# First values loaded in eight pieces by head to 64 partitions each, with the first loads' order and VectorE's first steps rearranged

## The chip, the cores and the metric

The kernel runs on one core of a Trainium2 chip. The metric is the device time of one execution in microseconds. Before the change it is 104.87 us, the median of three runs (104.6 to 105.11).

## The reference

A sketched polynomial attention, and behind it a two-layer block. All inputs and the output are float32.

```python
# q, k, v: (batch 4, heads 4, seq 1088, head_dim 32); S1, S2: (8, 32)
def phi(x):
    a = np.einsum('rd,bhsd->bhsr', S1, x)
    b = np.einsum('rd,bhsd->bhsr', S2, x)
    return np.einsum('bhsi,bhsj->bhsij', a, b).reshape(*x.shape[:-1], 64)
q_p, k_p = phi(q), phi(k)
kv = np.einsum('bhsf,bhsd->bhfd', k_p, v)
z = np.sum(k_p, axis=2)
x = einsum('bhsf,bhfd->bhsd', q_p, kv) / (einsum('bhsf,bhf->bhs', q_p, z)[..., None] + 1e-06)
# x as (4352 tokens, 128 = heads * head_dim); w_in: (128, 2048), w_out: (2048, 128)
h = x @ w_in
out = (h - np.tanh(h)) @ w_out
```

## The kernel before, in words

The four batches are worked through one after the other. A sequence of 1088 positions is cut into 34 blocks of 32, position `j * 34 + c` being row j of block c; a key or query tile holds (head, j) on 128 partitions and (block, dimension) along them. For each batch the kernel loads the keys (`kraw`), turns them in 32x32 blocks on VectorE (`kT`, two halves, L514), multiplies them on TensorE by the sketch (`kp`, L525) and turns the result (`kab`, L531). The products of the two sketches are `wk` (L545, in pieces on VectorE and GpSimd). TensorE sums `wk` times the values `vx` over the sequence (`sum`, L581); the result is spread by ScalarE (`kvz`, L591), turned by TensorE (`turn`, L601) and stored as the weights `ndw` (L608). The queries (`qraw`) are turned (`qT`, L620), projected (`qp`; L643 for the first 12 blocks, L660 for the others), normalized (`qab`, `au`, `dn`, `rd`, `an`), multiplied out (`qm`, L684), turned (`qt`, L691) and multiplied by `ndw` (`num`, L706). That gives `xT`, the input of the second part (L729).

The second part takes groups of 8 to 16 blocks: products with 16 slices of `w_in` (`h`, L778), tanh of the negative on ScalarE (`t`, L781), and the sum with 16 slices of `w_out` (`o`, L829). The linear share of the output comes from the product of the two weight matrices (`wp`, `whi`, `wlo`, L747 to L752, L821).

The order of the work is written out by hand: `ORDERS` lists the steps of each engine's program, `SESSIONS` the turns of the PSUM banks. `GATES` holds added dependences: `a<b` lets step a start after step b. Steps on SyncE are loads and stores in the order in which its queue issues them; ScalarE issues a few loads as well (`VENG` and `KENG` name which). In TensorE's list `~52`, `*4`, `^1` and the like stand for matmuls of constants, whose results nobody reads.

The tile `vx` has (block group ct, j) on its 128 partitions and, for each head, up to 9 blocks of 32 dimensions along them. The groups have 9, 9, 8 and 8 blocks (`KS`). Before the change `load_v` fills 32 partitions for all four heads with one load, `v0.0` to `v0.3` for the first batch. `sum0.0` (block places 0 to 3) and `sum0.4` (places 4 to 8) wait for all pieces of the first values. The load `wo0` of half of `w_out` is gated on `sum0.4`.

Of the kernel before, what the change touches and what calls it, by code (L numbers as in the profile page):

```python
# [14 lines left out]
NJB = DFF // 128  # L15
# [25 lines left out]
class Program:  # L41
# [241 lines left out]
k0.1 s1 act0 v0.2 v0.3 kap0 qab0 wq0u wic0 kvz0 ndw0 wic2 wic3 x0.0 t2 t3 t13 t11 t15 t14 t0 t1 t9 t5 t4 t12 t10 t8 t6
t7 x1.0 x1.2 t30 t22 t20 t18 t19 t32 t31 t47 t24 t16 t17 t42 t25 t23 t21 t29 t28 t27 t26 t39 t34 t38 t43 t46 t33 kvz1
t35 t40 t45 ndw1 t36 t44 t37 t41 t51 t49 t53 t48 t64 t50 t57 t52 t54 t59 t55 t65 t63 t58 t56 t60 t61 t62 t66 t67 t69
t68 kvz2 t72 t74 t70 ndw2 t78 t73 t71 t75 t76 t77 t84 t79 t87 t85 t80 t81 t109 t83 t90 t101 t88 t108 t82 t86 t93 t103
t89 t91 t105 t92 t94 t95 t96 kvz3 t111 t97 t98 ndw3 t110 t100 t99 t106 t104 t102 t112 t107 t116 t118 t114 t124 t122
t120 t128 t130 t126 t134 t132 t140 t138 t136 t146 t144 t142 t148 t150 t152 t154 t156 t158 out9.1 st9
# [13 lines left out]
s2 k0.0 q0.1 q0.0 q0.2 v0.1 v0.0 wi0 wi2 wi3 wi1 k1.0 wo0 wo1 wT q1.0 k2.0 v1.0 v1.1 v1.2 v1.3 st1.0.0 st1.0.3 q2.0
v2.2 v2.3 st0.0.2 st0.0.1 st0.0.3 st0.0.0 v2.0 st2.0.2 st2.0.3 v2.1 st1.0.1 v3.1 st2.0.0 st1.0.2 v3.3 st2.0.1 v3.0
k3.0 v3.2 st3.0.2 q3.0 st3.0.0 st3.0.1 st4.0.1 st3.0.3 st4.0.3 st5.2.2 st5.0.1 st5.2.3 st4.0.2 st5.2.0 st4.0.0 st5.0.0
st5.2.1 st6.0.1 st5.0.3 st6.0.3 st5.0.2 st7.0.2 st6.0.2 st7.4.2 st6.0.0 st7.4.1 st7.4.3 st7.0.0 st7.0.1 st7.4.0
st8.0.3 st8.0.0 st8.0.2 st7.0.3 st8.0.1
""",
}

# [10 lines left out]


GATES = """
id0<hm4.3 kTz0<hm4.3 kTz1<qT0.0 vz0<sel au1.0<bmask au1.1<bmask wqz<kp0 qTz0<hm4 qTz1<wq0 vz1<wq q0.0<hm2 v0.0<identb
v0.2<au1.1 v0.3<vz1 wi0<wkm wi1<qab0 wi2<wqz wi3<kTz1 q0.2<hm4 k1.0<qpu0 v1.0<o11 v1.1<h25 v1.2<t25 v1.3<o23
wo0<sum0.4 wo1<wic2 q1.0<t0 wic1<num0.0 woc0<kT1.0 wk0.29<wq0 qm0.2<dn0 wk1.12<o9 wk1.30<o13 k2.0<o9 v2.0<h64 v2.1<o35
v2.2<o4 v2.3<wk1.12 q2.0<qt2.2 au2<h23 an2<o22 qm2.2<t26 wk2.12<qab3 wk2.30<o33 k3.0<t66 v3.0<h49 v3.1<t50 v3.3<h60
q3.0<h30 wk3.12<o78 au4<o82 an4<t86 qm4.2<o86
"""


def bass_polysketch_attn__then__act_tanh_shrink_kernel(nc, q, k, v, S1, S2, moe_w_in, moe_w_out, out):
# [17 lines left out]
    def dve(n):  # L349
        return 45 + n / 0.96  # L350
# [70 lines left out]
    def constants():  # L421
        T = -9e5
        P.op("act0", "scalar", 1300, lambda e: e.copy(junk[:, :], nc.const_aps.tensor(1.0, [128, 1], BF16)), w=[("junk",)], prio=T)
        P.op("hm4", "vector", 70, lambda e: e.memset(hm4[:, :], 0.0), w=[("hm4",)], prio=T + 1)
        for h in range(H):
            P.op(f"hm4.{h}", "vector", 70, lambda e, h=h: e.memset(hm4[32 * h:32 * h + 32, h:h + 1], 1.0),
                 w=[("hm4",)], prio=T + 1)
        P.op("hm2", "vector", 80, lambda e: e.tensor_tensor(
            out=hm2[:, :], in0=hm4[:, 0:2], in1=hm4[:, 2:4], op=ALU.add), r=[("hm4",)], w=[("hm2",)], prio=T + 2)
# [15 lines left out]
        P.op("identb", "gpsimd", 250, lambda e: e.tensor_copy(identb[:, :], ident[:, :]), r=[("ident",)], w=[("identb",)], prio=T + 5)
# [23 lines left out]
    def load_v(b, eng, prio):  # L469
        i = b % 2  # L470
        src = v[b].rearrange("h (j c) d -> j h c d", j=32)
        for ct, (c0, n) in enumerate(KS):
            P.op(f"v{b}.{ct}", VENG.get((b, ct), eng), 0, lambda e, ct=ct, c0=c0, n=n: e.dma_start(
                out=vx[i][32 * ct:32 * ct + 32, :, 0:n, :].rearrange("j h t d -> j h (t d)"),
# [151 lines left out]
    def q_front(u, b, c0, nc_, early, bk):  # L626
# [4 lines left out]
        first = [c0 + sum(own[:ct]) for ct in range(4)]  # L631
        n = 4 * m
        cols = sorted({c for ct in range(4) for c in range(first[ct], min(first[ct] + m, 34))})
        need = [("qT", i, c) for c in cols] + ([("qTz", i)] if first[3] + m > 34 else [])
        if early:
            def project(x0, x1, base):
                def fn(e):
                    for t in range(m):
                        for c in range(2):
# [4 lines left out]
                    return ins  # L644
                return fn

            held = bank(f"qp{u}", bk)
            P.op(f"qp{u}", "tensor", pef(2 * m, 64, 64, 2), project(0, 16, 0), r=[("wq0",)] + need, w=held, ins=8 * m)
            pq = ps[:, bk, 0:16 * n].rearrange("p (n x) -> p n x", x=16)
            pu = ps[:, bk, 16 * n:24 * n].rearrange("p (n x) -> p n x", x=8)  # L650
            P.op(f"qab{u}", "scalar", act(16 * n), lambda e: e.copy(qab[ui][:, 0:n, 0:16], pq), r=held, w=[("qab", ui)])
            P.op(f"qpu{u}", "tensor", pef(2 * m, 64, 32, 2), project(16, 24, 16 * n), r=[("wq0u",)] + need, w=held, ins=8 * m)
        else:
            b0 = QBASE.get(u, 0)
            banks = range(b0, b0 + H)
# [1 line left out]
            def project(e):  # L657
# [100 lines left out]
    def layers(g, p0, nb, when):  # L758
# [2 lines left out]
        pace = PACE * n / 512  # L761
        slot = n_slot[0]
        n_slot[0] += NJB
        for jb in range(0, NJB, 2) if g in PAIRG else ():
            s = slot + jb
            b0, ts, at = (PBANKS if g not in ROWS else PBANKS[1:])[n_pair[0] % (len(PBANKS) - (g in ROWS))], s % TSLOTS, when + pace * jb
            n_pair[0] += 1
            for y in range(2):
# [3 lines left out]
            P.op(f"t{s}", "scalar", act(2 * n), lambda e, ts=ts, b0=b0: e.activation(  # L772
                out=tt[:, ts:ts + 2, 0:n], in_=ps[:, b0:b0 + 2, 0:n], func=AF.Tanh, scale=-1.0),
                r=bank(f"h{s}", b0, b0 + 1), w=[("t", ts), ("t", ts + 1)], prio=at)
        for jb in range(NJB) if g not in PAIRG else ():
            s = slot + jb
            bk, ts, at = 4 + s % NHB, s % TSLOTS, when + pace * jb
            P.op(f"h{s}", "tensor", pe(n), lambda e, jb=jb, bk=bk: e.matmul(  # L778
# [154 lines left out]
```

## Time and profile before

| what | value |
|---|---|
| median of the runs | 104.87 us (104.6 to 105.11) |
| the profiled execution: time, span from first to last instruction | 104.0 us, 102.2 us |
| TensorE matmul busy | 93.5 us (91%) |
| ScalarE busy | 79.6 us (78%) |
| VectorE busy | 54.8 us (54%) |
| GpSimd busy | 34.1 us (33%) |
| chain that ended last | TensorE 62%, GpSimd 11%, DMA 10%, VectorE 9% |
| DMA | 11.74 MB, mean 115 GB/s over the span |
| VectorE waiting for TensorE's sums of the second layer (L829) | 17.1 us |

A busy share is a mean over stages with different limits. The chain that ended last follows the work back from the last instruction to what released each step, and so tells which engine or load held the end in each stage. The page's row of DMA shares over 40 slices of the span shows the loads at nine tenths and more in the slices from 2.6 us on, at the start of the program, and far lower in the rest.

### The profile page before, as it was taken

To read this page: it belongs to the slowest core of one execution; us is meant where nothing else is said; L and a number is where in the kernel's file an instruction comes from. 1 tells how busy PE (TensorE), PEld (TensorE's weight loads), DVE (VectorE), ACT (ScalarE), POOL (GpSimd) and SP (SyncE) were. 2 spreads that over 40 slices of the span, in tenths; PEclk is the share of its full clock that TensorE was granted. 3 is DMA by queue.
4 is the path that set the end of the run, shared out by engine and by line. 5 is a ranking of instruction groups with operands and counts; after the bars stand their busy time and mean duration, and the time that the engine had idled before them with its cause. 6 is when DMAs were issued, how large, how long until landed. Compare 5 with 4: busy or idle time off the path is not lost.

```text
span 102.2 us, 3184 instructions
## 1 busy us (share of the span) xinstructions
PE 93.5 (91%) x1365; PEld 49.3 (48%) x1377; DVE 54.8 (54%) x95; ACT 79.6 (78%) x156; POOL 34.1 (33%) x41
## 2 busy tenths in 40 slices
PE   6978969999999989999999999999899999999950
PEld 6725642457444754433464344444443444456740
DVE  2589988885586765973086884830756020020210
ACT  2203579877998693999899779999776999999940
POOL 3138322834438950019980000569900000000000
PEclk9999999999999999999999999999999999999999
DMA  2999989954432139247579400130045003006242
GB/s 56 333 270 243 286 282 266 206 199 133 149 88 76 22 89 301 37 93 163 129 234 232 106 6 0 31 46 0 6 67 86 2 0 58 0 7 108 32 76 75
DMA packets 25949, 11.74 MB, mean 115 GB/s; under 512 B 19792, under 2 KB 24400, under 8 KB 25936
## 3 DMA queue, kind: packets, MB, share of 16 engines
q1 hardware_dynamic: 25320, 10.89, 44.0%
q10 hardware_dynamic: 616, 0.66, 2.3%
q8 instruction: 10, 0.16, 0.7%
q14 instruction: 3, 0.02, 0.1%
HBM read 8.79 MB, written 2.23 MB: 108 GB/s over the span
## 4 chain that ended last, share of the span: by engine, by line
PE 62%; POOL 11%; DMA 10%; DVE 9%; issue 3%; SPq 1%; POOLq 0%; DVEq 0%
PE ps L829 22%; PE ps L778 14%; PE ps L769 8%; POOL qp L684 8%; DMA w_out_f<-in_moe_w_out_dram 6%; PE ps L706 6%; DMA qraw<-in_q_dram 4%; PE ps L821 3%; DVE qpT L691 2%; PE ps L581 2%; PE ps L660 2%; PE ps L794 2%; DVE wk L545 2%; DVE qab L666 1%; DVE qT L620 1%
## 5 line engine op out<-in xcount | busy, mean ns | idle before, releaser
L781 ACT ACTIVATE tt<-ps 128x512 bf16<-128x512 f32 (+2 forms) x112 | 53.6, 549 | 7.8 <-PE ps L778 5.3
L829 PE MATMUL ps<-tt,w_out 128*128 128x512 bf16 (+3 forms) x141 | 39.7, 355 | 0.6 <-POOL w_out L738 0.3
L778 PE MATMUL ps<-xT,w_in 128*128 128x512 bf16 (+2 forms) x106 | 33.3, 353 | 1.7 <-ACT xT L729 0.6
L829 PEld LDWEIGHTS ps<-tt,w_out 128*128 128x128 bf16 x144 | 13.9, 99 | 12.2 <-ACT tt L781 0.8
L772 ACT ACTIVATE tt<-ps 128x1024 bf16<-128x1024 f32 (+2 forms) x24 | 18.6, 866 | 0.1
L778 PEld LDWEIGHTS ps<-xT,w_in 128*128 128x128 bf16 x112 | 10.2, 97 | 17.0 <-ACT tt L781 10.1
L684 POOL TENSOR_TENSOR qp<-an,qab 128x1152 f32<-128x1152 f32 (+2 forms) x8 | 15.4, 1926 | 1.9 <-DVE an L677 1.2
L691 DVE STREAM_TRANSPOSE qpT<-qp 128x1152 f32<-128x1152 f32 (+2 forms) x10 | 11.2, 1129 | 7.9 <-POOL qp L684 7.8
L834 DVE STREAM_TRANSPOSE osb<-ps 128x512 f32<-128x512 f32 (+3 forms) x9 | 5.8, 648 | 17.8 <-PE ps L829 17.1
L545 POOL TENSOR_TENSOR wk<-kab 128x384 f32<-128x384 f32 (+2 forms) x8 | 9.0, 1127 | 14.5 <-PE ps L829 14.0
L769 PE MATMUL ps<-xT,w_in 128*128 128x512 bf16 (+2 forms) x48 | 12.4, 335 | 0.0
L706 PE MATMUL ps<-qpT,ndw 32*32 32x288 f32 (+4 forms) x320 | 6.9, 352 | 0.4 <-DVE qpT L691 0.3
L729 DVE CAST xT<-ps 128x576 bf16<-128x576 f32 (+2 forms) x7 | 4.4, 682 | 4.7 <-PE ps L706 4.7
L769 PEld LDWEIGHTS ps<-xT,w_in 128*128 128x128 bf16 x48 | 4.4, 97 | 4.7 <-ACT tt L772 1.4
L671 POOL TENSOR_TENSOR au<-qab 128x288 f32<-128x288 f32 x3 | 2.4, 792 | 12.0 <-DVE qab L666 10.3
L514 DVE STREAM_TRANSPOSE kT<-kraw 128x512 f32<-128x512 f32 (+1 forms) x8 | 5.8, 720 | 0.8 <-DMA kraw<-in_k_dram 0.8
L620 DVE STREAM_TRANSPOSE qT<-qraw 128x1088 f32<-128x1088 f32 (+2 forms) x5 | 5.4, 1072 | 1.3 <-DMA qraw<-in_q_dram 1.3
L666 DVE STREAM_TRANSPOSE qab<-ps 128x1152 f32<-128x1152 f32 (+1 forms) x4 | 5.1, 1282 | 0.9 <-PE ps L660 0.7
L706 PEld LDWEIGHTS ps<-qpT,ndw 32*32 32x32 f32 x320 | 4.1, 103 | 2.9 <-DVE qpT L691 1.2
L581 PE MATMUL ps<-wk,vx 128*32 128x64 f32 x288 | 4.9, 220 | 0.5 <-DVE wk L545 0.5
L581 PEld LDWEIGHTS ps<-wk,vx 128*32 128x32 f32 x288 | 4.2, 110 | 1.4 <-issue 1.4
L416 PE MATMUL ps<-const-bfloat16-1.0 128*32 128x256 bf16 x77 | 3.9, 372 | 0.8 <-PEq L918 0.8
(82 smaller groups left out, 76.3 us busy)
## 6 DMA issues: line engine op xcount, KB each, us to landing
kraw<-in_k_dram SPq DMA_DIRECT2D x3, 544.0 KB, 4.1
qraw<-in_q_dram SPq DMA_DIRECT2D x3, 544.0 KB, 4.5
vx<-in_v_dram SPq DMA_DIRECT2D x8, 144.0 KB, 2.9
w_in_f<-in_moe_w_in_dram SPq DMA_DIRECT2D x4, 256.0 KB, 4.3
w_out_f<-in_moe_w_out_dram SPq DMA_DIRECT2D x2, 512.0 KB, 5.9
vx<-in_v_dram SPq DMA_DIRECT2D x6, 128.0 KB, 3.1
out_dram<-osb SPq DMA_DIRECT2D x12, 64.0 KB, 2.0
out_dram<-osb SPq DMA_DIRECT2D x12, 48.0 KB, 2.0
```

What stands on the lines that cost most here:

```text
L545: P.op(f"wk{b}.{n0}", eng, (dve if eng == "vector" else pool)(64 * n), lambda e, n0=n0, n1=n1, n=n, a_=a_: e.tensor_tensor(out=wk[0][:, n0 ...
L581: ins = e.matmul(ps[32 * h:32 * h + 32, SB, 0:64], vx[i][:, h, t, :], wk[0][:, 4 * t + h, :], start=(t == 0), stop=(t == 8), tile_position ...
L620: P.op(f"qT{b}.{lo}", "vector", dve(32 * (hi - lo)), lambda e: e.transpose(out=dst, in_=src), r=[("qraw", i, c) for c in range(lo, hi)], w ...
L666: P.op(f"qab{u}", "vector", dve(32 * n), lambda e: e.transpose(out=qab[ui][:, 0:n, :].rearrange("p (h t) x -> p h t x", h=H), in_=ps[:, b0 ...
L684: P.op(f"qm{u}.{h0}", eng, (pool if eng == "gpsimd" else dve)(64 * (n1 - n0)), lambda e, n0=n0, n1=n1, b_=b_: e.tensor_tensor(out=qp[ui][: ...
L691: P.op(f"qt{u}.{h0}", "vector", dve(64 * (n1 - n0)), lambda e, n0=n0, n1=n1: e.transpose(out=qpT[ui][:, n0:n1, :, :].rearrange("p n y j -> ...
L706: ins = e.matmul(ps[32 * h:32 * h + 32, ct, 0:32 * own[ct]], ndw[i][32 * ct:32 * ct + 32, y, 32 * h:32 * h + 32], qpT[ui][32 * ct:32 * ct ...
L769: P.op(f"h{s + y}", "tensor", pe(n), lambda e, jb=jb, b0=b0, y=y: e.matmul(ps[:, b0 + y, 0:n], w_in[:, 128 * (jb + y):128 * (jb + y) + 128 ...
L772: P.op(f"t{s}", "scalar", act(2 * n), lambda e, ts=ts, b0=b0: e.activation(out=tt[:, ts:ts + 2, 0:n], in_=ps[:, b0:b0 + 2, 0:n], func=AF.T ...
L778: P.op(f"h{s}", "tensor", pe(n), lambda e, jb=jb, bk=bk: e.matmul(ps[:, bk, 0:n], w_in[:, 128 * jb:128 * jb + 128], xT[:, t0:t0 + n], star ...
L781: P.op(f"t{s}", "scalar", act(n), lambda e, ts=ts, bk=bk: e.activation(out=tt[:, ts, 0:n], in_=ps[:, bk, 0:n], func=AF.Tanh, scale=-1.0), ...
L829: P.op(f"o{slot + jb}", "tensor", pe(n), lambda e, jb=jb, ts=ts: e.matmul(acc[:, 0:n], w_out[:, jb, :], tt[:, ts, 0:n], start=late and jb ...
```

## The change

The values of the first batch (`VHEADS`) are loaded in eight pieces, one for each head and each half of the partitions: 64 partitions of one head, two block groups of 32 partitions side by side. Four pieces go out on SyncE's queue and four on ScalarE's. The gates on these loads and on two of the query loads are removed (`q0.0<hm2`, `v0.0<identb`, `v0.2<au1.1`, `v0.3<vz1`, `q0.2<hm4`), as is the gate `kTz1<qT0.0` of a fill on GpSimd. The query pieces `q0.0` and `q0.1` are issued in the order of their blocks. VectorE turns both halves of the first keys and then copies the sketches (`wkm`, `wq`, `s2f`, `wq0`), turns the projected keys and then the queries. TensorE's two runs of constant matmuls at the start get three and four more. The zero fill behind `qT` is 64 columns wide instead of 32. The diff also holds further paths (`PAIR1`, `PSG`, `BU`, and a split turn of the queries) that no list or size of this kernel uses.

```diff
-VENG = {(0, 2): 'scalar', (0, 3): 'scalar'}
+VENG = {(0, 4): 'scalar', (0, 5): 'scalar', (0, 6): 'scalar', (0, 7): 'scalar'}
+VHEADS = (0,)
 ORDERS = {
     "tensor": """
-~52 sk ~25 kp0 *4 gram0 qp0 fold0 ...
+~55 sk ~29 kp0 *4 gram0 qp0 fold0 ...
     "scalar": """
-k0.1 s1 act0 v0.2 v0.3 kap0 qab0 ...
+k0.1 s1 act0 v0.4 v0.5 v0.6 v0.7 kap0 qab0 ...
     "vector": """
-hm4 hm4.0 hm4.1 hm4.2 hm4.3 hm2 sel bmask kT0.2 wkm wq kT0.0 s2f qT0.0 wq0 kab0 qT0.12 gm0 ...
+hm4 hm4.0 hm4.1 hm4.2 hm4.3 hm2 sel bmask kT0.2 kT0.0 wkm wq s2f wq0 kab0 qT0.0 qT0.12 gm0 ...
     "sync": """
-s2 k0.0 q0.1 q0.0 q0.2 v0.1 v0.0 wi0 wi2 wi3 wi1 k1.0 wo0 wo1 ...
+s2 k0.0 q0.0 q0.1 q0.2 v0.0 v0.1 v0.2 v0.3 wi0 wi2 wi3 wi1 k1.0 wo0 wo1 ...
 GATES = """
-id0<hm4.3 kTz0<hm4.3 kTz1<qT0.0 vz0<sel ... q0.0<hm2 v0.0<identb
-v0.2<au1.1 v0.3<vz1 wi0<wkm wi1<qab0 wi2<wqz wi3<kTz1 q0.2<hm4 k1.0<qpu0 ...
+id0<hm4.3 kTz0<hm4.3 vz0<sel ... wi0<wkm wi1<qab0 wi2<wqz
+wi3<kTz1 k1.0<qpu0 ...
 def load_v(b, eng, prio):
     i = b % 2
     src = v[b].rearrange("h (j c) d -> j h c d", j=32)
+    if b in VHEADS:
+        for x in range(2 * H):
+            h, (p0, c0, n) = x % H, ((0, 0, 9), (64, 18, 8))[x // H]
+            P.op(f"v{b}.{x}", VENG.get((b, x), eng), 0, lambda e, h=h, p0=p0, c0=c0, n=n: e.dma_start(
+                out=vx[i][p0:p0 + 64, h, 0:n, :].rearrange("p t d -> p (t d)"),
+                in_=v[b, h].rearrange("(j c) d -> j c d", j=32)[:, c0:c0 + 2 * n, :].rearrange("j (x t) d -> x j (t d)", x=2)),
+                w=[("vx", i)], sem=f"v{i}" + ("a" if (b, x) in VENG else ""), prio=prio, size=64 * 128 * n, also=True)
+        return
```

More of the change, by code (lines that the diff above doesn't have):

```diff
@@ L259 @@
 KENG = {(0, 1): 'scalar'}
-VENG = {(0, 2): 'scalar', (0, 3): 'scalar'}
+VENG = {(0, 4): 'scalar', (0, 5): 'scalar', (0, 6): 'scalar', (0, 7): 'scalar'}
 AENG = {2: 'gpsimd', 3: 'gpsimd', 4: 'gpsimd'}
+VHEADS = (0,)
+PAIR1 = ()
+PSG = ()
+BU = {}
 ORDERS = {
     "tensor": """
-~52 sk ~25 kp0 *4 gram0 qp0 fold0 *1 ^1 qpu0 sum0.0 sum0.4 *2 turn0 ^1 qp1 num0.0 num0.1 !1 h2 h3 h13 h11 h15 h1 h14
+~55 sk ~29 kp0 *4 gram0 qp0 fold0 *1 ^1 qpu0 sum0.0 sum0.4 *2 turn0 ^1 qp1 num0.0 num0.1 !1 h2 h3 h13 h11 h15 h1 h14
 h0 kp1 h9 h5 o0 h4 o1 o2 h12 gram1 o3 h10 h8 fold1 o4 o5 h6 h7 num1.0 num1.1 o6 o7 o8 o9 o10 h30 o11 h20 o12 o13 h22
@@ L282 @@
     "scalar": """
[L283 to L288, printed above, removed]
+k0.1 s1 act0 v0.4 v0.5 v0.6 v0.7 kap0 qab0 wq0u wic0 kvz0 ndw0 wic2 wic3 x0.0 t2 t3 t13 t11 t15 t14 t0 t1 t9 t5 t4 t12
+t10 t8 t6 t7 x1.0 x1.2 t30 t22 t20 t18 t19 t32 t31 t47 t24 t16 t17 t42 t25 t23 t21 t29 t28 t27 t26 t39 t34 t38 t43 t46
+t33 kvz1 t35 t40 t45 ndw1 t36 t44 t37 t41 t51 t49 t53 t48 t64 t50 t57 t52 t54 t59 t55 t65 t63 t58 t56 t60 t61 t62 t66
+t67 t69 t68 kvz2 t72 t74 t70 ndw2 t78 t73 t71 t75 t76 t77 t84 t79 t87 t85 t80 t81 t109 t83 t90 t101 t88 t108 t82 t86
+t93 t103 t89 t91 t105 t92 t94 t95 t96 kvz3 t111 t97 t98 ndw3 t110 t100 t99 t106 t104 t102 t112 t107 t116 t118 t114
+t124 t122 t120 t128 t130 t126 t134 t132 t140 t138 t136 t146 t144 t142 t148 t150 t152 t154 t156 t158 out9.1 st9
 """,
     "vector": """
-hm4 hm4.0 hm4.1 hm4.2 hm4.3 hm2 sel bmask kT0.2 wkm wq kT0.0 s2f qT0.0 wq0 kab0 qT0.12 gm0 wk0.8 wk0.0 wk0.16 au0 dn0
+hm4 hm4.0 hm4.1 hm4.2 hm4.3 hm2 sel bmask kT0.2 kT0.0 wkm wq s2f wq0 kab0 qT0.0 qT0.12 gm0 wk0.8 wk0.0 wk0.16 au0 dn0
 rd0 an0 qm0.0 wqu0 qt0.0 qt0.2 qab1 au1 dn1 rd1 kT1.0 an1 kT1.2 qm1.0 kab1 qt1.0 gm1 qt1.2 wqu1 wk1.24 wk1.0 qT1.0 whi
@@ L301 @@
     "sync": """
[L302 to L306, printed above, removed]
+s2 k0.0 q0.0 q0.1 q0.2 v0.0 v0.1 v0.2 v0.3 wi0 wi2 wi3 wi1 k1.0 wo0 wo1 wT q1.0 k2.0 v1.0 v1.1 v1.2 v1.3 st1.0.0
+st1.0.3 q2.0 v2.2 v2.3 st0.0.2 st0.0.1 st0.0.3 st0.0.0 v2.0 st2.0.2 st2.0.3 v2.1 st1.0.1 v3.1 st2.0.0 st1.0.2 v3.3
+st2.0.1 v3.0 k3.0 v3.2 st3.0.2 q3.0 st3.0.0 st3.0.1 st4.0.1 st3.0.3 st4.0.3 st5.2.2 st5.0.1 st5.2.3 st4.0.2 st5.2.0
+st4.0.0 st5.0.0 st5.2.1 st6.0.1 st5.0.3 st6.0.3 st5.0.2 st7.0.2 st6.0.2 st7.4.2 st6.0.0 st7.4.1 st7.4.3 st7.0.0
+st7.0.1 st7.4.0 st8.0.3 st8.0.0 st8.0.2 st7.0.3 st8.0.1
 """,
@@ L322 @@
 GATES = """
[L323 to L327, printed above, removed]
+id0<hm4.3 kTz0<hm4.3 vz0<sel au1.0<bmask au1.1<bmask wqz<kp0 qTz0<hm4 qTz1<wq0 vz1<wq wi0<wkm wi1<qab0 wi2<wqz
+wi3<kTz1 k1.0<qpu0 v1.0<o11 v1.1<h25 v1.2<t25 v1.3<o23 wo0<sum0.4 wo1<wic2 q1.0<t0 wic1<num0.0 woc0<kT1.0 wk0.29<wq0
+qm0.2<dn0 wk1.12<o9 wk1.30<o13 k2.0<o9 v2.0<h64 v2.1<o35 v2.2<o4 v2.3<wk1.12 q2.0<qt2.2 au2<h23 an2<o22 qm2.2<t26
+wk2.12<qab3 wk2.30<o33 k3.0<t66 v3.0<h49 v3.1<t50 v3.3<h60 q3.0<h30 wk3.12<o78 au4<o82 an4<t86 qm4.2<o86
 """
@@ L372, in bass_polysketch_attn__then__act_tanh_shrink_kernel @@
     kT = [sb(f"kT{i}", [128, 9, 4, 32]) for i in range(2)]
-    qT = [sb(f"qT{i}", [128, 35 * 32]) for i in range(2)]
+    qT = [sb(f"qT{i}", [128, 36 * 32]) for i in range(2)]
     vx = [sb(f"vx{i}", [128, H, 9, D]) for i in range(2)]
@@ L447, in constants @@
         for i in range(2):
-            P.op(f"qTz{i}", "gpsimd", 170, lambda e, i=i: e.memset(qT[i][:, 34 * 32:35 * 32], 0.0), w=[("qTz", i)], prio=T + 7)
+            P.op(f"qTz{i}", "gpsimd", 170, lambda e, i=i: e.memset(qT[i][:, 34 * 32:36 * 32], 0.0), w=[("qTz", i)], prio=T + 7)
         P.op("vz1", "gpsimd", 250, lambda e: e.memset(vx[1][64:128, :, 8, :], 0.0), w=[("vz", 1)], prio=T + 8)
@@ L615, in q_turned @@
         i = b % 2
+        if early and (hi - lo) % 4 == 2:
+            m = (hi - lo + 2) // 4
+            to = qT[i][:, 32 * lo:32 * (lo + 4 * m)].rearrange("p (t c j) -> p c t j", c=4, j=32)
+            for c, at, n in ((0, lo, m), (2, lo + 2 * m, m - 1)):
+                P.op(f"qT{b}.{at}", "vector", dve(64 * n), lambda e, c=c, at=at, n=n: e.transpose(
+                    out=to[:, c:c + 2, 0:n, :], in_=qraw[i][:, 32 * at:32 * (at + 2 * n)].rearrange("p (c t j) -> p c t j", c=2, j=32)),
+                    r=[("qraw", i, x) for x in range(at, at + 2 * n)], w=[("qT", i, x) for x in range(at, at + 2 * n)])
+            return
         dst, src = qT[i][:, 32 * lo:32 * hi], qraw[i][:, 32 * lo:32 * hi]
@@ L633, in q_front, with project @@
         cols = sorted({c for ct in range(4) for c in range(first[ct], min(first[ct] + m, 34))})
-        need = [("qT", i, c) for c in cols] + ([("qTz", i)] if first[3] + m > 34 else [])
+        need = [("qT", i, c) for c in cols] + ([("qTz", i)] if first[3] + m > 34 or (early and nc_ % 4) else [])
         if early:
-            def project(x0, x1, base):
+            def project(x0, x1, base, bk):
                 def fn(e):
@@ L645, in project @@
                 return fn
-            held = bank(f"qp{u}", bk)
-            P.op(f"qp{u}", "tensor", pef(2 * m, 64, 64, 2), project(0, 16, 0), r=[("wq0",)] + need, w=held, ins=8 * m)
+            held, hu, bu = bank(f"qp{u}", bk), bank(f"qp{u}", bk), bk
+            ub = 16 * n
+            if u in BU:
+                bu, ub = BU[u], 0
+                hu = bank(f"qp{u}", bu)
+            P.op(f"qp{u}", "tensor", pef(2 * m, 64, 64, 2), project(0, 16, 0, bk), r=[("wq0",)] + need, w=held, ins=8 * m)
             pq = ps[:, bk, 0:16 * n].rearrange("p (n x) -> p n x", x=16)
-            pu = ps[:, bk, 16 * n:24 * n].rearrange("p (n x) -> p n x", x=8)
+            pu = ps[:, bu, ub:ub + 8 * n].rearrange("p (n x) -> p n x", x=8)
             P.op(f"qab{u}", "scalar", act(16 * n), lambda e: e.copy(qab[ui][:, 0:n, 0:16], pq), r=held, w=[("qab", ui)])
-            P.op(f"qpu{u}", "tensor", pef(2 * m, 64, 32, 2), project(16, 24, 16 * n), r=[("wq0u",)] + need, w=held, ins=8 * m)
+            P.op(f"qpu{u}", "tensor", pef(2 * m, 64, 32, 2), project(16, 24, ub, bu), r=[("wq0u",)] + need, w=hu, ins=8 * m)
         else:
@@ L668, in q_front @@
                 in_=ps[:, b0:b0 + H, 0:32 * m].rearrange("p h (t j) -> p h t j", j=32)), r=bank(f"qp{u}", *banks), w=[("qab", ui)])
-            pq, pu, held = qab[ui][:, 0:n, :], qab[ui][:, 0:n, 16:24], []
+            pq, pu, held, hu = qab[ui][:, 0:n, :], qab[ui][:, 0:n, 16:24], [], []
         src = held + [("qab", ui)]
         P.op(f"au{u}", AENG.get(u, "vector"), (dve if u not in AENG else pool)(8 * n) + 30, lambda e: e.tensor_tensor(
-            out=au[ui][:, 0:n, 0:8], in0=qab[ui][:, 0:n, 0:8], in1=pu, op=ALU.mult), r=src, w=[("au", ui)], lock=not early)
+            out=au[ui][:, 0:n, 0:8], in0=qab[ui][:, 0:n, 0:8], in1=pu, op=ALU.mult), r=hu + src, w=[("au", ui)], lock=not early)
         P.op(f"dn{u}", "vector", dve(9 * n) + 30, lambda e: e.tensor_reduce(
@@ L763, in layers @@
         n_slot[0] += NJB
+        for jb, m in ((0, 2), (2, 1), (3, 2), (5, 1), (6, 2), (8, 1), (9, 2), (11, 1), (12, 2), (14, 1), (15, 1)) if g in PSG else ():
+            s = slot + jb
+            bk, ts, at = 4 if m == 2 or jb == 15 else 6, s % TSLOTS, when + pace * jb
+            for y in range(m):
+                P.op(f"h{s + y}", "tensor", pe(n), lambda e, jb=jb, bk=bk, y=y: e.matmul(
+                    ps[:, bk + y, 0:n], w_in[:, 128 * (jb + y):128 * (jb + y) + 128], xT[:, t0:t0 + n], start=True, stop=True),
+                    r=[("w_in", (jb + y) // 4)] + xs, w=bank(f"h{s}", bk + y), prio=at - 1000, ins=4)
+            P.op(f"t{s}", "scalar", act(m * n), lambda e, ts=ts, bk=bk, m=m: e.activation(
+                out=tt[:, ts:ts + m, 0:n], in_=ps[:, bk:bk + m, 0:n], func=AF.Tanh, scale=-1.0),
+                r=bank(f"h{s}", *range(bk, bk + m)), w=[("t", ts + y) for y in range(m)], prio=at)
+        for jb in range(0, NJB, 2) if g in PAIR1 else ():
+            s = slot + jb
+            bk, ts, at = 4 + (s // 2) % NHB, s % TSLOTS, when + pace * jb
+            for y in range(2):
+                P.op(f"h{s + y}", "tensor", pe(n), lambda e, jb=jb, bk=bk, y=y: e.matmul(
+                    ps[:, bk, n * y:n * y + n], w_in[:, 128 * (jb + y):128 * (jb + y) + 128], xT[:, t0:t0 + n], start=True, stop=True),
+                    r=[("w_in", jb // 4)] + xs, w=bank(f"h{s}", bk), prio=at - 1000, ins=4, also=y == 1)
+            P.op(f"t{s}", "scalar", act(2 * n), lambda e, ts=ts, bk=bk: e.activation(
+                out=tt[:, ts:ts + 2, 0:n], in_=ps[:, bk, 0:2 * n].rearrange("p (y n) -> p y n", y=2), func=AF.Tanh, scale=-1.0),
+                r=bank(f"h{s}", bk), w=[("t", ts), ("t", ts + 1)], prio=at)
         for jb in range(0, NJB, 2) if g in PAIRG else ():
@@ L774, in layers @@
                 r=bank(f"h{s}", b0, b0 + 1), w=[("t", ts), ("t", ts + 1)], prio=at)
-        for jb in range(NJB) if g not in PAIRG else ():
+        for jb in range(NJB) if g not in PAIRG + PAIR1 + PSG else ():
             s = slot + jb
```

## The prediction

> **What bounds the kernel now.** I read the chain of waits first. The program splits into an opening of about 14 us, in which loads arrive and the first batch's attention is prepared, and a long stage in which TensorE is nearly always busy. The change touches the opening alone, so its worth is read there. Columns: start, length, what held the chain.
>
> ```profile
> 2.07 3.98 DMA qraw<-in_q_dram
> ...
> 6.15 0.58 DVE qT L620
> ...
> 6.83 0.69 DVE kab L531
> 7.52 0.80 DVE qT L620
> ...
> 8.39 1.67 DVE wk L545 x3
> 10.06 0.08 issue
> 10.14 1.25 PE ps L581 x72
> ...
> 11.40 5.82 DMA w_out_f<-in_moe_w_out_dram
> ...
> 17.27 1.21 POOL w_out L738
> ...
> 18.61 1.52 POOL qp L684
> ...
> 20.15 0.98 DVE qpT L691
> ...
> 21.26 1.23 PE ps L706 x36
> ```
>
> Everything passes through the first sums (L581, "sum0") at 10.14 us. They stand in TensorE's program ahead of everything later, they need the key products `wk` and all of the first values `vx`, and the load of `w_out` is gated on their end. The chain names `wk`, but the values are as late. The `vx` view (SyncE's two issues, first and last start), its waits and the DMA list (KB, us from issue to landing) say so:
>
> ```profile
> L473 SPq DMA_DIRECT2D vx<-in_v_dram x2: 322/377/432, 3.1 to 5.6; - x2
> SPq L473 <- POOL identb L445: 2.0, 1, 2.0
> vx<-in_v_dram SPq DMA_DIRECT2D x1, 144.0 KB, 4.5
> ```
>
> The last piece is issued at 5.6 after a wait of 2.0 for `identb`, and lands at 5.6 + 4.5 = 10.1. So the landing of `vx` sets the start of sum0, as closely as VectorE does.
>
> What the transfer engines do, in windows (span, then five engines, clock, DMA share, GB/s; the last is a window that holds hardly anything but later `vx` packets):
>
> ```profile
> 1.00:2.00 1.00, 1.00 (x24) 0.86 (x20) 0.34 (x4) 0.20 (x1) 0.36 (x2) 1.00 0.30 35
> 3.00:4.00 1.00, 1.00 (x18) 0.56 (x10) 0.42 (x1) 0.28 (x2) 0.00 (x0) 1.00 1.03 364
> 5.00:10.00 5.00, 4.07 (x80) 2.12 (x71) 4.63 (x11) 0.91 (x3) 3.14 (x9) 1.00 0.98 258
> 43.50:43.90 0.40, 0.40 (x33) 0.08 (x1) 0.40 (x1) 0.40 (x2) 0.00 (x0) 1.00 0.72 245
> ```
>
> Share times 16 is the number of busy engines. One busy engine moves 364 / (1.03 x 16) = 22.1 GB/s at best, 245 / (0.72 x 16) = 21.3 with `vx` packets and little else, 258 / (0.98 x 16) = 16.5 with all sixteen crowded.
>
> **The change part by part.** SyncE's queue, with its waits; L464/L467 are the first queries, L473/L478 the first values. Before:
>
> ```order
> L464 DMA qraw<-in_q_dram 128x384
> L464 DMA qraw<-in_q_dram 128x256 [waits s_vector]
> L464 DMA qraw<-in_q_dram 128x448
> L473 DMA vx<-in_v_dram 32x4x288
> L473 DMA vx<-in_v_dram 32x4x288 [waits s_gpsimd]
> L479 DMA w_in_f<-in_moe_w_in_dram 128x512
> ```
>
> And after:
>
> ```order
> L467 DMA qraw<-in_q_dram 128x256
> L467 DMA qraw<-in_q_dram 128x384
> L467 DMA qraw<-in_q_dram 128x448
> L478 DMA vx<-in_v_dram 64x1x288 x4
> L490 DMA w_in_f<-in_moe_w_in_dram 128x512 [waits s_vector]
> ```
>
> Four value loads stand here and four more on ScalarE's queue, none waiting, instead of two and two with three gates. The bytes are the same, 8 x 64 rows of 1152 or 1024 bytes = 557 kB. The waits that go would bring the last issue forward from 5.6 to about 5. But the shape goes too. Before, both sides of a value load had an outermost step of 32 rows. Now the destination has 64, and the source is written `"j (x t) d -> x j (t d)"` with x=2: its outermost step has **two** entries. I take it that a transfer is dealt to engines by the outermost step that both sides share, so that each of the eight pieces is carried by two engines, and always the same two. No row of before has a step of two. The nearest is the load of `s`, with eight rows where all others have 32 or 128, and it alone is listed without a landing:
>
> ```profile
> kraw<-in_k_dram SPq DMA_DIRECT2D x1, 288.0 KB, 3.1
> kraw<-in_k_dram ACTq DMA_DIRECT2D x1, 256.0 KB, 2.8
> qraw<-in_q_dram SPq DMA_DIRECT2D x1, 224.0 KB, 4.7
> qraw<-in_q_dram SPq DMA_DIRECT2D x1, 192.0 KB, 3.9
> ...
> qraw<-in_q_dram SPq DMA_DIRECT2D x1, 128.0 KB, 4.0
> ...
> s<-in_S_dram SPq DMA_DIRECT2D x1, 4.0 KB
> s<-in_S_dram ACTq DMA_DIRECT2D x1, 4.0 KB
> ```
>
> That is a hint, not a proof, that a short outermost step completes differently; the ends are two engines (this forecast) and sixteen (first rival), and I take two because the step itself is two. [...]
>
> **The landing.** Each of the two engines carries its sixteenth of keys and queries first (1088 KB / 16 = 69.6 kB), then half of the values, 278.5 kB. Both queues issue early enough (by about 6 us) that these engines never run dry. At 21.3 GB/s that is 3.3 + 13.1 us. Traffic begins at 1.7 (share 0.30 in the window from 1 to 2), so the last value lands at 18.1 instead of 10.06, **+8.0 us**. At 22.1 GB/s it is 17.4 (+7.4), at 16.5 it is 22.8 (+12.7). I take 21.3: with fourteen engines done early, the two are hardly crowded.
>
> **TensorE after the pause.** These rows stand around sum0:
>
> ```profile
> 9.13 0.54 PE L643 MATMUL ps<-wq,qT 128*64 128x32 f32 x12
> 11.83 0.44 PE L601 MATMUL ps<-ident,kvz 128*128 128x128 f32 x2
> 12.31 0.61 PE L660 MATMUL ps<-qT,wq 32*32 32x192 f32 x32
> 12.83 1.00 PE L706 MATMUL ps<-qpT,ndw 32*32 32x96 f32 x64
> 13.87 0.48 ACT L729 CAST xT<-ps 128x384 bf16<-128x384 f32 x1
> ```
>
> TensorE would now idle from 9.7 (9.13 + 0.54) to 18. Its only long pause in this trace is the one before the start, and the same dummy matmul ran at 2.97 / 52 = 57 ns then and 0.91 / 25 = 36 ns later, though the clock column reads 1.00 in both (span, TensorE, its weight loads, clock, DMA share, GB/s):
>
> ```profile
> 0.70:4.20 3.50, 2.97 (x52) 2.19 (x52) 1.00 0.68 214
> 4.30:5.40 1.10, 0.91 (x25) 0.65 (x25) 1.00 0.97 291
> ```
>
> From sum0 to the first `xT` are 1.25 + 0.44 + 0.61 + 1.00 = 3.3 us of TensorE. Bounds: 0, and all of it at 57/36, +1.9. A slow stretch as long as at the start (3.5 us) does 3.5 x 36/57 = 2.2 us of work: I take **+1.3**. [...]
>
> **What comes back.** `w_out` needed 5.82 us from issue to landing in the crowd, and the chain runs through it to POOL's products, the turn and L706 at 21.26. Behind sum0 the crowd is thinner, but the two engines still owe the `w_in` and key pieces queued behind the values. ScalarE's tanh sequence is the next bound; it lost only this to the chain:
>
> ```profile
> 20.28 1.66 ACT L781 ACTIVATE tt<-ps 128x384 bf16<-128x384 f32 x4 [0.25 <-PE ps L778]
> 22.58 0.81 ACT L729 CAST xT<-ps 128x384 bf16<-128x384 f32 x2 [0.64 <-PE ps L706]
> ```
>
> So 0 to -0.9; I take **-0.4**.
>
> **VectorE's order.** `kT` is turned keys, `wq` and `s2f` sketches, `qT` turned queries. Before:
>
> ```order
> L514 STREAM_TRANSPOSE kT<-kraw 128x2x8x32
> L496 TENSOR_TENSOR wkm<-ps,hm 128x32
> L502 COPY wq<-ps 128x4x16
> L514 STREAM_TRANSPOSE kT<-kraw 128x2x9x32
> L504 TENSOR_TENSOR s2f<-ps,bmask 128x128
> L620 STREAM_TRANSPOSE qT<-qraw 128x4x3x32
> L499 TENSOR_TENSOR wq<-ps,hm 128x4x16
> L531 STREAM_TRANSPOSE kab<-ps 128x18x2x16
> L620 STREAM_TRANSPOSE qT<-qraw 128x704
> ```
>
> And after:
>
> ```order
> L525 STREAM_TRANSPOSE kT<-kraw 128x2x8x32
> L525 STREAM_TRANSPOSE kT<-kraw 128x2x9x32
> L507 TENSOR_TENSOR wkm<-ps,hm 128x32
> L513 COPY wq<-ps 128x4x16
> L515 TENSOR_TENSOR s2f<-ps,bmask 128x128
> L510 TENSOR_TENSOR wq<-ps,hm 128x4x16
> L542 STREAM_TRANSPOSE kab<-ps 128x18x2x16
> L639 STREAM_TRANSPOSE qT<-qraw 128x4x3x32
> L639 STREAM_TRANSPOSE qT<-qraw 128x704
> ```
>
> The second key half moves ahead of the sketches, and `kab` no longer stands behind the first queries.
>
> ```profile
> 4.84 0.77 DVE L514 STREAM_TRANSPOSE kT<-kraw 128x576 f32<-128x576 f32 x1
> 5.66 0.72 PE L525 MATMUL ps<-kT,wkm 64*32 64x288 f32 x16 [0.22 <-DVE kT L514]
> ```
>
> The keys could be projected from 5.3 instead of 5.66, but seven more dummy matmuls (0.3 us) stand before that, so `kab` starts at 6.3 to 6.5 and the last `wk` ends between 9.8 and 10.3 (6.3 to 6.5, plus 0.69 + 0.58 + 0.80 + 1.67 and gaps), against 10.06. Under the values' wait this is worth **0**; without that cover it is worth -0.25 to +0.25. The removed gates of GpSimd, the wider zero fill of `qT` and the swapped query pieces (both are needed by the same turn) also lie under that wait: 0.
>
> **The sum.** 8.0 + 1.3 - 0.4 + 0 = +8.9 us on the profiled execution's 104.0 (span 102.2 and 1.8 around it): 112.9. The median of the runs, 104.87, lies 0.9 above that execution, so I forecast 113.8.
>
> **The rivals.** *Sixteen engines after all (or a different pair for each piece)*: then the values land by about 9.5 and sum0 starts with its first two `wk` pieces, near 9.6. VectorE's order then rules, -0.4 to +0.25, about 104.7 on the median: not slower. For it: 32-row loads spread well now. Against it: the step of two. It decides if the values land before 10. [...]
>
> **How the numbers follow.** Forecast 0.85, two pairs 0.06, sixteen 0.09. The bounds of the forecast's terms give +7.4 + 0 - 0.9 = 6.5 to 12.7 + 1.9 = 14.6, or 111.4 to 119.5; I trim the crowded end, since all sixteen are never crowded that long, and leave room below for faster rows: 110.0 to 118.0. A measurement of this kernel can tell 0.5% (0.5 us) from no change. The sixteen-engine case splits into 0.04 faster and 0.05 the same; slower is 0.91.
>
> **What would show it.** Right: eight value loads landing 10 us or more after issue, DMA share near 2/16 from about 8 to 17 us, L581 starting near 18 with a long wait on a DMA, matmuls behind it at about 1.5 times their length, and the stage behind unchanged. [...]

## The result and the profile after

The changed kernel takes 114.73 us (114.14 to 115.22, 4 runs); the kernel before took 104.99 beside it. The ratio is 1.0939, 95% interval 1.0851 to 1.1027: slower, as forecast (113.8, range 110.0 to 118.0). The profiled execution is the longest of the four, 115.22 us with a span of 113.4. In all ratios of this document only executions without the chip's occasional slowdown count (in the second job below, 6 of the 23 of the kernel before), while medians count all, so a ratio need not be the quotient of two medians.

The DMA list of the first 20 us (KB each, us from issue to landing):

```profile
w_in_f<-in_moe_w_in_dram SPq DMA_DIRECT2D x4, 256.0 KB, 9.3
...
vx<-in_v_dram SPq DMA_DIRECT2D x4, 72.0 KB
...
vx<-in_v_dram ACTq DMA_DIRECT2D x4, 64.0 KB
qraw<-in_q_dram SPq DMA_DIRECT2D x1, 224.0 KB, 7.0
...
s<-in_S_dram SPq DMA_DIRECT2D x1, 4.0 KB
```

The eight value loads now stand without a landing, as only the loads of `s` did before. The last query piece takes 7.0 us to land where it took 4.7. Windows of the changed kernel (span, engines, clock, DMA share, GB/s):

```profile
5.00:6.00 1.00, 1.00 (x24) 0.72 (x21) 0.81 (x5) 0.00 (x0) 0.39 (x2) 1.00 0.56 185
...
7.00:8.00 1.00, 0.89 (x16) 0.13 (x2) 0.00 (x0) 0.00 (x0) 0.00 (x0) 1.00 0.14 49
...
11.00:12.00 1.00, 0.87 (x15) 0.43 (x12) 1.00 (x3) 0.23 (x2) 0.29 (x1) 1.00 0.14 44
...
16.00:17.00 1.00, 0.00 (x0) 0.00 (x0) 0.00 (x0) 0.00 (x0) 0.00 (x0) 0.50 0.89 288
...
19.00:20.00 1.00, 0.17 (x8) 0.20 (x12) 0.00 (x0) 0.00 (x0) 0.00 (x0) 0.50 0.13 50
```

From 7 to 12 us the share is 0.13 to 0.14 and 44 to 49 GB/s move, where before, from 5 to 10, it was 0.98 and 258. Two engines of sixteen are 0.125. From 12.5 to 18 the others come back with `w_in` and the next keys, then the share falls to 0.13 again (19 to 21). The chain of waits of the opening:

```profile
5.26 0.89 SPq L478
...
6.19 13.55 DMA vx<-in_v_dram
19.74 0.09 issue
19.83 2.15 PE ps L592 x72
...
25.15 0.49 ACT xT L752
...
32.05 1.16 PE ps L729 x36
```

The queries' load has given its place in the chain to the values, which land at 19.74 us instead of about 10.1. The same stage in order of time:

```profile
6.68 1.21 PE L536 MATMUL ps<-kT,wkm 64*32 64x288 f32 x16
...
8.95 4.45 SPq L490 DMA_DIRECT2D w_in_f<-in_moe_w_in_dram  x4
...
10.52 1.74 DVE L556 TENSOR_TENSOR wk<-ps,kab 128x512 f32<-128x512 f32 x3
...
19.83 2.15 PE L592 MATMUL ps<-wk,vx 128*32 128x64 f32 x72 [7.96 <-DMA vx<-in_v_dram]
...
22.74 0.64 PE L612 MATMUL ps<-ident,kvz 128*128 128x128 f32 x2
```

The sums in the kernel before, from its timeline:

```profile
10.14 1.21 PE L581 MATMUL ps<-wk,vx 128*32 128x64 f32 x72 [0.47 <-DVE wk L545]
```

TensorE waits 7.96 us for the values and then works at half clock (0.50 in the window rows above): the sums take 2.15 us where they took 1.21. VectorE's last `wk` piece was done at 12.3, long before.

### The profile page after: what moved, and what is told of

Same layout as the page of the kernel before. It is cut to its first block, busy times and chain, and to the rows that moved or that the text cites. A ratio compares the mean times of both kernels' runs of the same rounds, so it can differ in the third digit from the quotient of the medians.

```text
span 113.4 us, 3201 instructions
## 1 busy us (share of the span) xinstructions
PE 97.1 (86%) x1372; PEld 51.7 (46%) x1384; DVE 54.8 (48%) x95; ACT 79.4 (70%) x156; POOL 34.5 (30%) x41
## 4 chain that ended last, share of the span: by engine, by line
PE 60%; DMA 12%; POOL 8%; DVE 6%; SPq 4%; issue 3%; ACT 2%; POOLq 0%
PE ps L872 20%; PE ps L821 13%; DMA vx<-in_v_dram 12%; PE ps L812 7%; PE ps L729 6%; POOL qp L707 6%; PE ps L592 3%; PE ps L864 3%; SPq L478 3%; PE ps L683 2%; DVE qpT L714 2%; ACT tt L824 2%; PE ps L837 2%; POOL au L694 1%; DVE qab L689 1%
## 5 line engine op out<-in xcount | busy, mean ns | idle before, releaser
L872 PEld LDWEIGHTS ps<-tt,w_out 128*128 128x128 bf16 x144 | 13.9, 99 | 11.5 <-ACT tt L824 1.0
L821 PEld LDWEIGHTS ps<-xT,w_in 128*128 128x128 bf16 x112 | 10.2, 97 | 17.4 <-ACT tt L824 10.4
L707 POOL TENSOR_TENSOR qp<-an,qab 128x1152 f32<-128x1152 f32 (+2 forms) x8 | 15.9, 1991 | 2.9 <-DVE an L700 2.1
L714 DVE STREAM_TRANSPOSE qpT<-qp 128x1152 f32<-128x1152 f32 (+2 forms) x10 | 11.2, 1126 | 7.8 <-POOL qp L707 7.8
L592 PE MATMUL ps<-wk,vx 128*32 128x64 f32 x288 | 5.8, 243 | 8.0 <-DMA vx<-in_v_dram 8.0
L592 PEld LDWEIGHTS ps<-wk,vx 128*32 128x32 f32 x288 | 5.1, 125 | 8.9 <-issue 8.9
L758 ACT CAST w_in<-w_in_f 128x512 bf16<-128x512 f32 x3 | 1.8, 619 | 9.1 <-DMA w_in_f<-in_moe_w_in_dram 9.1
L729 PE MATMUL ps<-qpT,ndw 32*32 32x288 f32 (+4 forms) x320 | 7.1, 352 | 0.3 <-DVE qpT L714 0.3
L419 PE MATMUL ps<-const-bfloat16-1.0 128*32 128x256 bf16 x84 | 5.1, 417 | 0.8 <-PEq L961 0.8
```

Source lines behind the costliest of these rows:

```text
L592: ins = e.matmul(ps[32 * h:32 * h + 32, SB, 0:64], vx[i][:, h, t, :], wk[0][:, 4 * t + h, :], start=(t == 0), stop=(t == 8), tile_position ...
L707: P.op(f"qm{u}.{h0}", eng, (pool if eng == "gpsimd" else dve)(64 * (n1 - n0)), lambda e, n0=n0, n1=n1, b_=b_: e.tensor_tensor(out=qp[ui][: ...
L714: P.op(f"qt{u}.{h0}", "vector", dve(64 * (n1 - n0)), lambda e, n0=n0, n1=n1: e.transpose(out=qpT[ui][:, n0:n1, :, :].rearrange("p n y j -> ...
L729: ins = e.matmul(ps[32 * h:32 * h + 32, ct, 0:32 * own[ct]], ndw[i][32 * ct:32 * ct + 32, y, 32 * h:32 * h + 32], qpT[ui][32 * ct:32 * ct ...
L872: P.op(f"o{slot + jb}", "tensor", pe(n), lambda e, jb=jb, ts=ts: e.matmul(acc[:, 0:n], w_out[:, jb, :], tt[:, ts, 0:n], start=late and jb ...
```

## The experiments

The experiments ran in two jobs, each with the kernel before beside them. The first had the old loads, the sixteen loads in the changed kernel, the half of the new loads and TensorE kept busy, and 105.64 us for the kernel before. The second had the others, and 106.05. Across jobs ratios are therefore compared, not microseconds. Each profile shows one execution. The code edits are shown in part, with `...` where lines are left out.

**The new loads alone, in the kernel before.** With `VHEADS` and its branch, the three value gates out, all else as before:

```diff
-VENG = {(0, 2): 'scalar', (0, 3): 'scalar'}
+VENG = {(0, 4): 'scalar', (0, 5): 'scalar', (0, 6): 'scalar', (0, 7): 'scalar'}
+VHEADS = (0,)
...
-k0.1 s1 act0 v0.2 v0.3 kap0 ...
+k0.1 s1 act0 v0.4 v0.5 v0.6 v0.7 kap0 ...
...
-s2 k0.0 q0.1 q0.0 q0.2 v0.1 v0.0 wi0 ...
+s2 k0.0 q0.1 q0.0 q0.2 v0.0 v0.1 v0.2 v0.3 wi0 ...
```

> The kernel before with the eight new value loads and the three value gates removed, and nothing else: VectorE's order, the query gates and the dummy matmuls are those of before. Theory (the new loads carry the whole loss, because the other edits lie under the wait for the values): 114 to 115.3 us, first sums at about 19.7 us. Rival (VectorE's order and the added dummies contribute): below 113.5 us.

It took 114.22 us, ratio 1.0856 (1.0756 to 1.0956), which overlaps that of the whole change. Its chain:

```profile
5.46 13.73 DMA vx<-in_v_dram
19.19 0.09 issue
19.28 2.15 PE ps L590 x72
```

The loads alone give nearly the same wait (7.8 us), a landing 0.55 us earlier and the same slow sums. Whether the other edits add anything to them can't be told from these runs.

**The old loads in the changed kernel.**

```diff
-VHEADS = (0,)
+VHEADS = ()
-k0.1 s1 act0 v0.4 v0.5 v0.6 v0.7 kap0 ...
+k0.1 s1 act0 v0.2 v0.3 kap0 ...
-s2 k0.0 q0.0 q0.1 q0.2 v0.0 v0.1 v0.2 v0.3 wi0 ...
+s2 k0.0 q0.0 q0.1 q0.2 v0.0 v0.1 wi0 ...
```

> The changed kernel with the first values loaded in the four pieces of before (32 partitions, four heads), all other edits kept. Theory (two transfer engines carry the new pieces): the first sums start near 10 us, the DMA share stays near 1 up to 14 us, and the time is 104.5 to 105.2 us. Rival (VectorE's order, the removed gates or the added dummy matmuls carry part of the loss, since in the changed kernel the first key projection began at 6.68 instead of 5.66 us): 106 us or more, first sums at 11 us or later.

106.67 us, ratio 1.0125 (1.0061 to 1.019). Most of the loss is gone, but not all, and the number is the rival's. The six times spread from 106.02 to 107.51 us, so that the last 1% stands on few runs. In its `vx` view (ns min/median/max, first and last start; us to landing) the first sums start at 11.6:

```profile
L592 PE MATMUL ps<-wk,vx x72: 216/219/243, 11.6 to 12.6; 128*32 128x64 f32 x72
...
DMA to landing us min/median/max: 4.3/5.7/6.6
```

The first key projection of this profile starts late and is slow, 1.21 us from 6.68 on, as in the changed kernel, and the sums no longer wait for the values. So without the values' wait the remaining edits were not free in this form. The next run keeps the same order, starts its key projection and its sums as late, and does not show that loss, so neither the order by itself nor the late start is what cost 1%. What did stays open.

**Sixteen loads, by head to 32 partitions.** Both sides have 32 as outermost step:

```diff
-            for x in range(2 * H):
-                h, (p0, c0, n) = x % H, ((0, 0, 9), (64, 18, 8))[x // H]
+            for x in range(4 * H):
+                h, ct = x % H, x // H
+                c0, n = KS[ct]
...
-                    out=vx[i][p0:p0 + 64, h, 0:n, :].rearrange("p t d -> p (t d)"),
-                    in_=...[:, c0:c0 + 2 * n, :].rearrange("j (x t) d -> x j (t d)", x=2)),
+                    out=vx[i][32 * ct:32 * ct + 32, h, 0:n, :].rearrange("p t d -> p (t d)"),
+                    in_=...[:, c0:c0 + n, :].rearrange("j t d -> j (t d)")),
```

> The changed kernel with sixteen pieces by head to 32 partitions each, so that both sides of every load have 32 as their outermost step; the bytes, the rows of 1152 and 1024 bytes and the split by head stay. Theory (the outermost step of two is the cause): first sums at 10 to 10.5 us, a landing is listed for these loads, 104.5 to 105.5 us. Rival (many small pieces by head are the cause, with their issues and completions): 108 us or more, since there are twice as many pieces.

105.72 us, ratio 1.0009 (0.9973 to 1.0044): no difference from before. The list has landings again:

```profile
vx<-in_v_dram SPq DMA_DIRECT2D x8, 36.0 KB, 3.7
...
vx<-in_v_dram ACTq DMA_DIRECT2D x8, 32.0 KB, 3.7
```

The DMA share is back at 0.99 in the window from 5 to 6 us. Twice as many pieces, the same bytes and row lengths, and 8.5% less time than the changed kernel by the ratios (1.0009 / 1.0939). Splitting by head is not the cause; the rival falls. The sums started later than expected, at 11.5, behind a late rise of TensorE's clock in this execution (the first key projection took 1.21 us from 6.68 on; below).

**Half of the new loads.** The lower 64 partitions as changed, the upper in two loads of 32 partitions:

```diff
-            for x in range(2 * H):
+            for x in range(H):
...
+            for x, ct in ((4, 2), (5, 3)):
+                (the load of 32 partitions and four heads of before)
```

> The changed kernel with the new pieces for the lower 64 partitions only (four loads of 64 x 1152 bytes, 295 kB); the upper 64 come in two loads of 32 partitions as before. Theory (two engines, at the rate seen in the changed kernel): each of the two carries 147 kB of these values instead of 278 kB, so the last one lands 131 kB / 21 GB/s = 6.2 us earlier, at about 13 us, TensorE's pause is about 3 us instead of 8, and the time is 107 to 109 us. Rival (a fixed cost of a load of this shape, not its bytes): the same 114 to 115 us, or the full return to 105.

110.5 us, ratio 1.0457 (1.0393 to 1.0521). The chain and a window:

```profile
5.09 9.02 DMA vx<-in_v_dram
14.12 0.25 issue
14.36 1.21 PE ps L598 x72
```

```profile
16.00:17.00 1.00, 1.00 (x14) 0.54 (x20) 0.00 (x0) 0.18 (x2) 0.00 (x0) 0.50 0.31 104
```

The dose counts: half of the bytes on two engines, and the landing moves from 19.7 to 14.1; the rival of a fixed cost falls. I expected 13 and 107 to 109, and TensorE's pause, 2.96 us, came as expected. The step is 5.6 us instead of 6.2. The two engines also carry their sixteenth of the other 262 kB, 16 kB, which I had left out: (131 - 16) kB / 21 GB/s = 5.5 us. The rest of the miss in the landing is that 13 was counted from about 19.2 and not from 19.7. I had also left out that the clock still falls, here at 15.7 us, after the pause was over and the first sums were done at full clock.

**A step of three.** Four loads to 96 partitions for three block groups, the rest in loads of 32 partitions:

```diff
+            for h in range(H):
...
+                    out=vx[i][0:96, h, 0:8, :].rearrange("p t d -> p (t d)"),
+                    in_=...[:, 0:27, :].rearrange("j (x t) d -> x j t d", x=3)[:, :, 0:8, :].rearrange("x j t d -> x j (t d)")),
```

> The changed kernel with the values of the first three block groups loaded in four pieces by head to 96 partitions, whose source has an outermost step of three entries (393 kB); the fourth group and the ninth blocks come in loads of 32 partitions. Theory (the outermost step that both sides share sets the number of engines): three engines carry them, the DMA share stands near 3/16 = 0.19 on its low stretch instead of 0.13, each engine has 131 kB, and the last value lands about 1 us before that of the run with half of the new pieces (147 kB each, landing at 14.1), near 13 us. Rival (any such shape falls to two engines): share 0.13, 197 kB each, landing near 16 us.

A single execution, 109.28 us; its time is not weighed, only its landing and its shares. Chain, and windows:

```profile
5.46 8.24 DMA vx<-in_v_dram
13.74 2.15 PE ps L596 x72
```

```profile
14.00:15.00 1.00, 1.00 (x48) 1.00 (x44) 0.00 (x0) 0.62 (x1) 0.00 (x0) 0.50 0.20 74
15.00:16.00 1.00, 0.89 (x36) 0.79 (x28) 0.00 (x0) 0.04 (x1) 0.00 (x0) 0.50 0.19 71
```

The values land at 13.7, where two engines would have needed until about 16 by the same sum; that is 0.4 us before the run with half of the new loads, not the 1 us expected. And what is left queued behind them, `w_in` and keys, runs at a share of 0.19 to 0.20: three engines of sixteen (0.1875), as it ran at 0.13 behind the step of two. So source steps of 2, 3 and 32 went with two, three and about all sixteen engines (shares of 0.13 to 0.14, 0.19 to 0.20 and 0.99). The destinations had 64, 96 and 32 partitions with them. No run changes the source's step and keeps the destination, so that the source decides alone is not shown; the step that both sides share, as the prediction assumed, fits all three.

**TensorE kept busy.**

```diff
-... ^1 qpu0 sum0.0 sum0.4 ...
+... ^1 qpu0 *30 sum0.0 sum0.4 ...
```

> The changed kernel with thirty more dummy matmuls (512 columns, 6.5 us at full rate) between the projection of the first queries and the first sums; nothing else moves. Theory (the pause also slows TensorE): the granted clock stays at 1.00 past 13.5 us, the first sums take 1.2 instead of 2.15 us, and the time falls by 1.0 to 1.6 us to about 113.3. Rival (the slow stretch is hidden under other waits): 114.5 to 115.0, as before.

113.14 us, ratio 1.0734 (1.0687 to 1.0781), below the changed kernel's interval. From its timeline:

```profile
19.79 1.21 PE L592 MATMUL ps<-wk,vx 128*32 128x64 f32 x72
...
23.88 0.48 ACT L752 CAST xT<-ps 128x384 bf16<-128x384 f32 x1 [0.50 <-PE ps L729]
```

The sums are back at 1.21 us, and from them to the first `xT` are 4.09 us instead of 5.32. The lead stays to the end: the last copy (L851) starts at 107.94 instead of 109.19. So the slow stretch costs about 1.2 us by itself, on top of the wait. The ratios differ by more, 1.9%, but their intervals allow anything from 0.7% to 3.2%. The clock did not stay at 1.00, as I had expected: it was at half from 11.4 to 14.8 us, and full again when the sums began. Ahead of that fall TensorE had been idle for only 1.7 us (8.7 to 10.4). The last dummy ended just where the sums begin; whether fewer dummies would give more was not tried.

**Fewer dummies, and sixteen loads in the old order.** The sixteen loads with `~52` and `~25`, and the same loads in the kernel before without its value gates.

> The sixteen pieces of 32 partitions with the changed order, and with the dummy counts of before (52 and 25 instead of 55 and 29). Theory (the seven added dummy matmuls stand ahead of the first key projection, and hold the opening whenever TensorE's clock is late to rise): 0.2 to 0.4 us below the run with sixteen pieces and 55 and 29, which had 105.72. Rival (the dummies are hidden): the same within 0.2 us.

> The kernel before with sixteen ungated value loads by head to 32 partitions, its own order otherwise. If the landing of the values at 10.05 us held the first sums there, they now start up to 0.5 us earlier and the time is 104.6 to 105.3 beside 105.0 to 105.6 for before. If the key products held them as well, no change.

105.58 us, 1.0009 (0.996 to 1.0058), and 105.79 us, 1.0005 (0.9945 to 1.0065). Neither can be told from the kernel before, so neither theory of these two is decided, and no version here beats it. In the profile of the second the first sums started at 10.7, later than in the profile of before (10.14), behind a late rise of the clock (the first key projection took 1.21 us from 6.33 on; below).

## Why the prediction was right

By its own steps, in microseconds on the profiled executions:

| step | forecast | measured |
|---|---|---|
| start of the first sums | +8.0 | 10.14 to 19.83: +9.7 |
| sums to first `xT` (clock) | +1.3 | 3.73 to 5.32: +1.6 |
| `xT` to L706/L729 of the next queries | -0.4 | 7.39 to 6.90: -0.5 |
| the rest of the span | 0 | 80.9 to 81.35: +0.4 |
| sum | +8.9 | +11.2 |

The 0.4 of the rest lies behind the last copy. From L706/L729 to that copy (98.59 and 109.19) are 77.3 and 77.1 us, so the stage behind the opening is unchanged, as forecast.

The time came out nearer than the steps. The steps were 2.3 us short on the profiled pair, but the medians differ by 9.7 us, 0.8 more than the 8.9 forecast: the profiled execution of before lies 1.0 below its median and that of after 0.5 above. That part of the closeness is luck.

*Two engines.* Shown, by the share of 0.13 to 0.14, by the dose (half of the new loads, 14.1 instead of 19.7) and by the step of three (0.19). The hint, a load without a landing, held: the new value loads are listed like `s`. So the sign of a landing 10 us or more after issue is read from the chain: issued at 6.19, landed 13.55 us later. That the outermost step sets the number of engines was the author's assumption; the shares here for steps of 2, 3 and 32 (0.13, 0.19 and 0.99) agree with it. Which engines these are, the views don't show.

*The landing was sized 1.6 us too early.* The rate was right; the beginning and the end were not. I had the two engines finish keys and queries first and begin with the values at 1.7 + 3.3 = 5.0 us. In the trace's packets the two run side by side: rows of values (1024 bytes, from ScalarE's queue) start at 5.5, and the last row of queries (1792 bytes) ends at 9.0. The order does not change the sum, since each engine has to move 69.6 + 278.5 = 348 kB before the last value is through. But by 7 us each had moved only about 86 kB, worked out from the rows still missing, and not 5.3 us x 21.3 GB/s = 113 kB, which is 1.3 us of work. The other 262 kB took until the end of the last value row at 19.3, which is 21.3 GB/s. From there to the landing at 19.74 are 0.45 us, which I had left out.

*The clock* was right in kind and near in size. The stretch is 1.6 us longer, for 1.3 forecast, and 1.2 of it go when TensorE is kept busy; the other 0.4 stay at full clock. Each sum took 0.31 us instead of 0.22, 1.4 times, and all 72 took 1.8 times as long, for the 1.5 named as a sign.

*Cover.* VectorE's order and the dummies were costed at nothing while the values are late: the new loads alone take the same time as the whole change, within their intervals. The uncovered price of -0.25 to +0.25 us is not settled: the ratios are +1.25% with the old loads and +0.1% with sixteen.

*One sign was only half right.* I expected a share near 2/16 from 8 to 17 us. It stood there from 7 to 12 and again from 19 on; between, `w_in` and keys used the other engines (shares of 0.48 to 1.11 from 12 to 18). These came late because SyncE's issues were held (below).

The rivals: sixteen engines falls with the share. Two pairs, one for each queue, had a chance of 0.06 and falls too: by the trace's packets value rows of both queues were moving from 8.7 us on, and up to 12 the share stayed at 0.13 to 0.14, two engines and not four.

## What to carry to other kernels

Read the outermost step of both sides of a load before its bytes: here a step of two left the transfer on two engines (share 0.13 to 0.14), and the time was near half of all bytes queued on the two, divided by one engine's rate (348 kB at 21.3 GB/s are 16.3 us; the last value landed 18.0 us after traffic began). A low, flat DMA share while something waits for a load is the sign; here share times sixteen gave the step, two (0.13 to 0.14) and three (0.19 to 0.20). Such a load can cost twice where TensorE waits for it, here 9.7 us as a later start and 1.2 to 1.6 us as slow matmuls behind it.

## What the runs showed of the hardware that was not expected

**The issue itself was held.** In the changed kernel SyncE's value loads took this long to issue (ns min/median/max):

```profile
L478 SPq DMA_DIRECT2D vx<-in_v_dram x4: 662/1150/2717, 3.1 to 6.2; - x4
...
L490 SPq DMA_DIRECT2D w_in_f<-in_moe_w_in_dram x4: 430/513/2858, 8.9 to 13.0; - x4
```

Before, the two took 322 to 432 ns. The first `w_in` load then went out at 8.95 instead of 5.92 us, and its own issue is the one of 2858 ns; its first packets start only at 12.45. With half of the new loads the longest value issue took 855 ns, with sixteen loads 429 ns. What holds the issue was not tried.

**The rise of TensorE's clock moves from run to run.** The clock column reads 1.00 at the start in all profiles, but the trace's clock records begin only with the first rise: at 4.25 us in the profile of before, 4.53 with TensorE kept busy, 10.06 in the changed kernel and 8.12 in the old order with sixteen loads. So the column tells nothing ahead of the first record. The first key projection, the same 16 matmuls, took 0.72 us at 5.66 in the profile of before and 0.72 at 5.72 with TensorE kept busy, and 1.21 us at 6.68 in the changed kernel. The 25 dummies ahead of it, first in the profile of before, then in the old order with sixteen loads, with the projection of the latter:

```profile
4.49 0.95 PE L416 MATMUL ps<-const-bfloat16-1.0 128*32 128x256 bf16 x25
...
4.72 1.68 PE L417 MATMUL ps<-const-bfloat16-1.0 128*32 128x256 bf16 x25
...
6.33 1.21 PE L535 MATMUL ps<-kT,wkm 64*32 64x288 f32 x16
```

In six of the ten profiles the rise came at 8.1 to 10.1 us, in the other four at 4.0 to 4.5. Where it was late, the first key projection started 0.7 to 1.0 us later than in the profile of before and took 0.5 us longer. That may be part of the spread of the runs; the link was not tried.
